# Output parts taken out of the matmul chain, and the third tile in pairs of block pairs

## The chip, the cores and the metric

The kernel runs on one core of a Trainium2 chip. The metric is the device time of one execution in microseconds (us), the median of several runs. TensorE is called PE here, VectorE DVE, ScalarE ACT, GpSimd POOL, and SyncE, which issues the transfers, SP.

## The reference

Attention inside chunks of 64 positions gives x, and x goes through a layer of two weight matrices with h*cos(h) between them, everything in f32:

```python
scores = scale * np.matmul(q_c, k_c.transpose(0, 1, 2, 4, 3))   # 8 x 8 heads, 9 chunks of 64, head size 64
scores = scores - np.max(scores, axis=-1, keepdims=True)
attn = np.exp(scores)
attn = attn / (np.sum(attn, axis=-1, keepdims=True) + 1e-09)
out = np.matmul(attn, v_c)
...
h = x @ w_in                       # x: 4608 x 512, w_in: 512 x 2048
g = h * np.cos(h)
return (g @ w_out).astype(np.float32)   # w_out: 2048 x 512
```

## The kernel before

The 4608 tokens are nine tiles of 512. Every f32 operand of the large products is split into a high and a low part, and a product is made of three matmuls: high by high, high by low, low by high. The products h = x w_in are made chunk by chunk (16 chunks `fc` of 128 hidden units), g = h cos(h) is made on ACT and DVE, split into g_hi (ACT, a cast) and g_lo (DVE or POOL, a subtraction), and multiplied by w_out into four accumulators `acc0` to `acc3`, one for each 128 tokens of the tile. One such step for one chunk and one accumulator is an output part (`out_part`, L1183): three matmuls of 128x512.

The first two tiles are made chunk by chunk. From the third tile on (`FAST = 2`) h of a block of 2x2 is made by seven products instead of eight, in Strassen's manner (A11, S3, S2, A12, A22, S1, S4), with sums and differences of x and of w_in; h is then put together with copies between banks (ACT) and additions (DVE). The third tile does this on its own two halves of 256 tokens: `single_pair` (L1630, called eight times) makes two chunks, with products of 256 columns in the halves of two PSUM banks. The later tiles are taken two at a time, with products of 512 columns: `wide_pair` (L1695) makes two chunks of both tiles; the g of the second tile of the two goes to DRAM (`gathered`) and comes back in `second_tile` (L1772).

The combinations of w_in are in DRAM (`combo`) and are streamed through seven rooms in SBUF, `w_in5` to `w_in11`, with two combinations to a room. `load_two` (L1060) fills a room with one transfer of 512 KB; in the third tile only rooms 5 to 8 are filled again (`KEPT_ROOMS`), and `product` (L1129) asks for the next filling behind the second product on a room. SP issues all transfers in one order.

What runs when: all work is written down as pieces (engine, length, what it waits for), and a list planner (`placed`, L322, called by `in_order`, L415) sorts the pieces of all engines once, by a due time for each piece from a table of numbers (`DUE_SECOND` for the stretch with the third tile and the two after it, `DUE_NEXT` for the next tiles, `DUE_LAST` for the last two). The instructions are then written in that order, and each engine keeps to it. The pieces of PE with 128-row operands are a chain: `pe` (L1555) makes each wait for the one before it, so that their order is the order in which the code makes them, and only the scores and weighted sums of the attention (matmuls of 64x64, in groups) are free to move among them. Output parts are links of this chain: `outs(n)` (L1582) puts the next n of the waiting output parts in at places that the code names, by the tuples of `PLAN` (L48) and by the arguments `after` of `single_pair` and `wide_pair`. An output part waits for g_lo of its chunk and, where it begins an accumulator, for the copy that empties that accumulator.

g_hi and g_lo have three rooms in turn (`parts_of_g`, L1592): the split of a chunk waits until the output parts on the chunk three before it are done. `chain` (L1610) makes g: a rounding on ACT, a turn on DVE, the sine on ACT, a product on DVE. `weighted_now` (L1887) puts the weighted sums of a later tile into the list.

## Time and profile before

| what | us |
|---|---|
| median of three runs | 792.22 |
| these runs | 791.0, 792.22, 794.23 |
| the profiled execution's own time | 789.22 |
| its span, first to last instruction | 787.5 |
| PE busy | 771.1 (98%) |
| DVE busy | 574.0 (73%) |
| ACT busy | 474.6 (60%) |
| POOL busy | 307.7 (39%) |

The profile is of one execution, on the only core. A time at the start of a row of the timeline counts from the span's start; what stands in brackets behind a row is how long the engine had been idle ahead of it, and which instruction ended the wait. Matmuls are pipelined: a row of a single matmul shows its whole passage, and the next one begins before that has ended. The third tile and the attention of the tiles after it lie at about 200 to 290 us, the later tiles from there to the end; the order of the instructions on PE is the same in both kernels up to about 200 us.

### The profile page before, as it was taken

The numbers are of one execution on the slowest core, as the hardware profiler recorded it, in microseconds if no ns is written. First come the engines' busy times: TensorE is split into PE (matmuls) and PEld (weight loads), VectorE is DVE, ScalarE is ACT, GpSimd is POOL, SyncE is SP. The second block draws the span as 40 slices with busy tenths as digits, with TensorE's granted clock in tenths as the row PEclk, the third lists the DMA queues.
The fourth block names the chain that finished last, engine by engine and source line by source line (L and its number), as shares of the span: only waits on it lengthen the run. The fifth ranks groups of instructions, "written<-read, shape, count | busy, mean of one in ns | idle before, by whom it ended". The sixth has DMA issues, their size and how long they took to land.

```text
span 787.5 us, 15182 instructions
## 1 busy us (share of the span) xinstructions
PE 771.1 (98%) x5818; PEld 672.4 (85%) x5818; DVE 574.0 (73%) x908; ACT 474.6 (60%) x874; POOL 307.7 (39%) x243
## 2 busy tenths in 40 slices
PE   7999999999999999999999999999999999999998
PEld 6788887888889988888888888888888888888887
DVE  6988888998898787884887868876888564463521
ACT  6999975555877666655654456544754465554422
POOL 3555537866734382211235731121245512131200
PEclk9999999999999999999999999999999999999999
DMA  9993706386886657646656349547463265553431
GB/s 343 411 416 114 242 1 235 132 318 220 310 271 198 218 188 243 239 134 217 213 150 211 117 168 322 184 150 253 145 203 108 61 222 171 190 165 128 157 98 67
DMA packets 71896, 156.18 MB, mean 198 GB/s; under 512 B 7184, under 2 KB 21776, under 8 KB 71824
## 3 DMA queue, kind: packets, MB, share of 16 engines
q1 hardware_dynamic: 71824, 155.22, 57.6%
q8 instruction: 46, 0.75, 0.4%
q14 instruction: 26, 0.21, 0.1%
HBM read 117.44 MB, written 37.75 MB: 197 GB/s over the span
## 4 chain that ended last, share of the span: by engine, by line
PE 82%; ACT 5%; DMA 5%; DVE 5%; issue 2%; POOL 0%; SPq 0%; ACTq 0%; DVEq 0%; POOLq 0%
PE acc L495 42%; PE h L495 31%; PE a L495 9%; DMA w_out<-in_w_out_dram 3%; DVE w L571 1%; ACT w L576 1%; DMA w_in<-in_w_in_dram 1%; ACT half L578 1%; DMA gathered<-w_in 1%; DMA kt<-in_kT_dram 1%; DVE m L716 0%; ACT g L895 0%; ACT g L893 0%; ACT w_out L512 0%; ACT e L728 0%
## 5 line engine op out<-in xcount | busy, mean ns | idle before, releaser
L495 PE MATMUL acc<-w_out,g_hi 128*128 128x512 f32 x1124 | 335.0, 380 | 0.0
L495 PEld LDWEIGHTS acc<-w_out,g_hi 128*128 128x128 f32 x1124 | 209.4, 189 | 29.0
L495 PE MATMUL acc<-w_out,g_lo 128*128 128x512 f32 x562 | 212.8, 379 | 0.9 <-POOL g_lo L516 0.9
L516 POOL TENSOR_TENSOR g_lo<-g,g_hi 128x512 fp32r<-128x512 f32 x75 | 108.1, 1443 | 266.0 <-ACT g_hi L512 123.2
L495 PE MATMUL h<-x,w_in 128*128 128x512 f32 (+1 forms) x864 | 199.8, 358 | 2.9 <-DVE g L1158 1.8
L495 PEld LDWEIGHTS h<-x,w_in 128*128 128x128 f32 x864 | 149.6, 190 | 24.3 <-DVE g L1158 3.0
L495 PE MATMUL h<-w_in,w_in 128*128 128x512 f32 (+1 forms) x576 | 135.9, 354 | 0.8 <-ACT h L1142 0.6
L495 PEld LDWEIGHTS acc<-w_out,g_lo 128*128 128x128 f32 x562 | 106.2, 189 | 16.4 <-POOL g_lo L516 1.3
L495 PEld LDWEIGHTS h<-w_in,w_in 128*128 128x128 f32 x576 | 99.5, 190 | 13.4 <-ACT h L1142 0.8
L512 ACT CAST g_hi<-g 128x512 fp32r<-128x512 f32 x99 | 61.2, 620 | 51.3 <-PE acc L495 32.1
L1151 DVE SCALAR_TENSOR_TENSOR g<-g,h 128x512 f32<-128x512 int32 (+1 forms) x40 | 23.1, 577 | 68.5 <-ACT g L1148 68.0
L495 PE MATMUL a<-x,w_in 128*128 128x512 f32 x288 | 70.3, 380 | 0.5 <-DVE w_in L720 0.3
L495 PEld LDWEIGHTS a<-x,w_in 128*128 128x128 f32 x288 | 54.1, 189 | 9.2 <-PE h L495 1.3
L516 DVE TENSOR_TENSOR g_lo<-g,g_hi 128x512 fp32r<-128x512 f32 x41 | 35.8, 874 | 26.0 <-ACT g_hi L512 25.4
L1155 ACT ACTIVATE g<-g 128x512 f32<-128x512 f32 (+1 forms) x72 | 41.5, 581 | 16.9 <-DVE g L1151 16.7
L1142 ACT COPY h<-h 128x512 f32<-128x512 f32 (+1 forms) x40 | 19.4, 486 | 51.7 <-PE h L495 41.3
L516 POOL TENSOR_TENSOR e<-e,z 128x512 f32<-128x512 f32 x13 | 16.9, 1308 | 44.0 <-DVE z L770 33.9
L1145 DVE TENSOR_TENSOR w_in<-h,w_in 128x512 f32<-128x512 f32 (+1 forms) x40 | 22.6, 582 | 15.4 <-PE h L495 10.6
L1155 ACT ACTIVATE w_in<-w_in 128x512 f32<-128x512 f32 x48 | 29.8, 628 | 5.4 <-DVE w_in L1151 5.3
L1158 DVE TENSOR_TENSOR g<-w_in,g 128x512 f32<-128x512 f32 x32 | 28.8, 899 | 3.5 <-ACT g L1155 2.5
L1148 ACT ACTIVATE g<-h 128x512 int32<-128x512 f32 (+1 forms) x40 | 20.5, 512 | 16.9 <-PE h L495 16.4
L571 DVE SCALAR_TENSOR_TENSOR w<-w,half 128x512 uint32<-128x512 uint32 x32 | 27.5, 862 | 3.9 <-ACT w L576 2.9
(205 smaller groups left out, 1166.6 us busy)
## 6 DMA issues: line engine op xcount, KB each, us to landing
w_in<-combo SPq DMA_DIRECT2D x112, 512.0 KB, 4.0
combo<-w_in SPq DMA_DIRECT2D x56, 256.0 KB, 3.3
gathered<-w_in SPq DMA_DIRECT2D x48, 256.0 KB, 2.5
qt<-in_qT_dram SPq DMA_DIRECT2D x36, 256.0 KB, 4.8
kt<-in_kT_dram SPq DMA_DIRECT2D x36, 256.0 KB, 5.1
w_in<-in_w_in_dram SPq DMA_DIRECT2D x16, 512.0 KB, 9.3
w_out<-in_w_out_dram SPq DMA_DIRECT2D x16, 512.0 KB, 9.6
w_in<-gathered SPq DMA_DIRECT2D x24, 256.0 KB, 2.9
```

The source lines that it names most:

```text
L495: kept(nc.tensor.matmul(*args, **kw))
L512: kept(nc.scalar.copy(out=out, in_=in_))
L516: kept(eng.tensor_tensor(out, a, b, op=op))
L571: kept(nc.vector.scalar_tensor_tensor(bits, bits, 3, low, op0=ALU.logical_shift_left, op1=ALU.bitwise_or))
L576: lambda: kept(nc.scalar.activation(w(), upper.bitcast(F32), AF.Prelu, scale=2.0 ** -(MORE // 8), alpha=-(2.0**32))),
L578: lambda: kept(nc.scalar.activation(low, lower, AF.Copy, scale=LOWEST)),
L1142: kept(nc.scalar.copy(out=out, in_=in_))
L1145: kept(nc.vector.tensor_tensor(out, a, b, op=ALU.add))
L1148: kept(nc.scalar.activation(g.bitcast(I32), h, AF.Identity, bias=0.25, scale=0.5 / math.pi))
L1151: kept(nc.vector.scalar_tensor_tensor(g, g.bitcast(I32), -2.0 * math.pi, h, op0=ALU.mult, op1=ALU.add))
L1155: kept(nc.scalar.activation(g, g, AF.Sin, bias=0.5 * math.pi))
L1158: kept(nc.vector.tensor_tensor(g, h, g, op=ALU.mult))
```

## The change

It has two parts, and new due tables for the last three stretches (1062 numbers before and 1010 now in the first of them), of which a line each:

```diff
 DUE_SECOND = (
-    -12.85, 2.21, 2.31, 3.75, 7.22, 3.78, 4.82, 4.73, 34.21, 4.92, 3.46, 22.89, 82.26, 18.21, 88.69, 755.07,
...
+    -34.98, 8.25, 2.5, -17, -0.46, -35.35, 120.61, -10.98, -53.72, 39.57, 9.53, 28.58, -9.06, 26.34, 20.94,
...
```

First, an output part is a piece of its own that waits only for its g_lo and for its accumulator. Which part is the first or the last of its accumulator is counted as the parts are made (`added`), and the copy out waits for all parts of the accumulator. `outs()` puts in all that wait; no place is named any more, in the third tile or in the wide pairs:

```diff
     def out_piece(t, fc, sub, half=None):
-        p = pe(
-            0.648 if half is None else 0.336, lambda: out_part(t, fc, sub, half), low_of.get((t, fc)),
-            acc_free.get(sub) if fc == first_fc(t) else None,
+        p = piece(
+            PE, 0.648 if half is None else 0.336, lambda: out_part(t, fc, sub, half), low_of.get(made_of(t, fc, sub)),
+            acc_free.get(sub), main=True,
         )
-        spent.setdefault((t, fc), []).append(p)
-        if fc == last_fc(t):
+        spent.setdefault(made_of(t, fc, sub), []).append(p)
+        made = asked_out.setdefault((t, sub), {None: [], 0: [], 1: []})
+        made[half].append(p)
+        to_come[t, sub, half] = to_come.get((t, sub, half), NFC if t else LAG) - 1
+        if half is not None:
+            if len(made[half]) == 2:
+                piece(ACT, 0.4, lambda: finish(t, sub, acc[sub], True, ACT, half), *made[None], *made[half])
+        elif not to_come[t, sub, half]:
...
-    def outs(n):
-        for _ in range(n):
...
+    def outs(n=None):
+        for _ in range(len(queue) if n is None else n):
             out_piece(*queue.popleft())
...
-        while any(q[:2] == back for q in queue):
-            outs(1)
```

Second, `two_pairs` (called four times) stands in for `single_pair`. It makes each of the seven products for two block pairs, in the two halves of one bank, so that the copies, additions, roundings, turns, sines and products on ACT and DVE take 512 columns at a time; the fourth bank is `a0`, the copy of d lies in `x0_3`, and two of the four g in `x0_2`:

```diff
-    def single_pair(k, after):
+    def two_pairs(q):
...
+        def prod(j, out, *deps, begin=None):
+            for i in range(2):
+                def go(i=i):
+                    if begin and not i:
+                        v[out] = begin()
+                    product(
+                        14 * q + 2 * j + i, v[out][:, i * HALF : (i + 1) * HALF], halves_x[j][:, 0], halves_x[j][:, 1],
+                        bool(begin) and not i,
+                    )
+                done[j] = product_piece(14 * q + 2 * j + i, 0.672, go, *(() if i else deps))
+            return done[j]
...
+        prod(A11, "a", *of(ha), begin=h_bank)
+        cb = piece(ACT, 0.6, copy_b, done[A11], *of(hb))
+        prod(S3, "d", *of("a1"), begin=lambda: bank("a", 1))
+        cd = piece(ACT, 0.6, copy_d, done[S3], *of("differences"))
+        prod(S2, "b", cb)
+        cc = piece(ACT, 0.6, copy_c, done[S2], *of("a0"))
+        prod(A12, "a", cb)
+        prod(A22, "c", cc)
+        prod(S1, "b", cc)
+        addc = piece(DVE, 0.69, add_c, done[A22], cd, *of("h2"))
+        addb = piece(DVE, 0.69, lambda: add(v["h3"], v["b"], v["ds"]), done[S1], cd, addc)
+        prod(S4, "b", addb)
...
+        for g, m, odd, half in (("g1", m1, 0, 0), ("g2", m2, 1, 0), ("g3", m3, 1, 1), ("g4", m4, 0, 1)):
+            low = parts_of_g(FAST, (q, odd, half), lambda g=g: v[g], m)
...
+            queue.extend((FAST, 4 * q + 2 * i + odd, 2 * half + sub) for i in range(2) for sub in range(2))
+            outs()
         return done
```

For this a room of the third tile holds the same combination of two block pairs, and `load_two` fills it with two transfers of 256 KB (56 in all) where one of 512 KB stood (28); the other 84 fillings stay as they were:

```diff
-            load(room.bitcast(F32), combos[i % len(combos)].rearrange("p n h d -> p (n h d)"))
+            if i < len(combos):
+                q, j = divmod(i, 7)
+                for n in range(2):
+                    load(room.bitcast(F32)[:, n * TOK : (n + 1) * TOK], combo(2 * q + n, j).rearrange("p h d -> p (h d)"))
+            else:
+                load(room.bitcast(F32), combos[i % len(combos)].rearrange("p n h d -> p (n h d)"))
```

The plan of the third tile, the rooms of x, and the second tile of two:

```diff
 PLAN = [
-    2, "scores", 2, "queries", (2, 0, 1, 1), (3, 0, 2, 3), (1, 0, 2, 2), "values", "scores 2", 3, (3, 0, 2, 3),
-    (3, 0, 2, 2), (1, 0, 3, 2), "weighted", 3, (1, 0, 2, 2), "weighted 2", 3, (3, 0, 2, 3),
+    "scores", "queries", "pair", "values", "scores 2", "pair", "weighted", "pair", "weighted 2", "pair",
 ]
 
-WIDE_X = ("x0_0", "x0_1", "x0_2", "x0_3", 13, 14, 15)
+WIDE_X = ("x0_0", "x0_1", 13, 14, 15, "x0_2", "x0_3")
...
-            while len(queue) > 8:
-                outs(1)
+            outs(max(0, len(queue) - 8) if t < NT - 1 else None)
+            if t < NT - 1 and fc == NFC // 2:
+                weighted_now(t + 2)
```

PE has 4668 matmuls in both kernels, with the same numbers of 256 and of 512 columns; only their banks and their order change. ACT has 37 instructions fewer and DVE 6, and SP has 28 more.

The order on PE is shown at three places. In its rows `h`, `a0` and `a1` are banks of products, `g_hi` and `g_lo` the parts of g, a number behind a name is that of the buffer, and `x3` means three alike in a row. The first place is the beginning of the third tile's products, just behind 200 us. Before, on PE, where the second two chunks begin:

```order
L495 MATMUL h_2832<-x1_1_2265,w_in5_2593 128x256 x6
L495 MATMUL h_2832<-x1_2_2266,w_in5_2593 128x256 x6
L495 MATMUL acc0_2789<-w_out0_599,g_hi_2749 128x512 x2
L495 MATMUL acc0_2789<-w_out0_599,g_lo_2750 128x512
L495 MATMUL h_2857<-x1_3_2267,w_in6_2644 128x256 x6
L495 MATMUL h_2832<-x1_0_2268,w_in6_2644 128x256 x6
L495 MATMUL h_2857<-w_in0_2269,w_in7_2667 128x256 x6
L495 MATMUL h_2857<-w_in1_2270,w_in7_2667 128x256 x6
L495 MATMUL acc1_2807<-w_out0_599,g_hi_2749 128x512 x2
L495 MATMUL acc1_2807<-w_out0_599,g_lo_2750 128x512
L495 MATMUL acc2_2817<-w_out0_599,g_hi_2749 128x512 x2
L495 MATMUL acc2_2817<-w_out0_599,g_lo_2750 128x512
```

Now, on PE, where the first four chunks begin, on the same parts of x:

```order
L491 MATMUL h_2626<-x1_1_2270,w_in5_1910 128x256 x12
L491 MATMUL acc1_2242<-w_out14_1491,g_hi_2438 128x512 x2
L491 MATMUL acc1_2242<-w_out14_1491,g_lo_2439 128x512
L491 MATMUL acc0_2238<-w_out13_1418,g_hi_2362 128x512 x2
L491 MATMUL acc0_2238<-w_out13_1418,g_lo_2363 128x512
L491 MATMUL a1_2666<-x1_2_2271,w_in6_2057 128x256 x12
L491 MATMUL h_2684<-x1_3_2272,w_in7_2060 128x256 x12
L491 MATMUL h_2626<-x1_0_2273,w_in8_2224 128x256 x12
L491 MATMUL a0_2718<-w_in0_2274,w_in9_2227 128x256 x12
L491 MATMUL h_2684<-w_in1_2275,w_in10_2389 128x256 x12
L491 MATMUL acc1_2242<-w_out15_1467,g_hi_2460 128x512 x2
L491 MATMUL acc1_2242<-w_out15_1467,g_lo_2461 128x512
```

Before, output parts stand between products that come one to four at a time, six matmuls each; now fourteen of these products (a row of x12 is two of them) come with few output parts between them, and those parts are of any accumulator and chunk that is ready.

The second place is the first group of scores behind the first of these products: `kt` and `qt` are keys and queries, and rows of one bank alternate with rows of the other. Before, on PE, the first rows of a group of 32, and its end, which is followed at once by the next 32:

```order
L495 MATMUL acc0_2789<-w_out3_859,g_hi_2850 128x512 x2
L495 MATMUL acc0_2789<-w_out3_859,g_lo_2851 128x512
L495 MATMUL h_2937<-kt_2562,qt_2561 64x64
L495 MATMUL a0_2938<-kt_2562,qt_2561 64x64
...
L495 MATMUL h_2937<-kt_2566,qt_2565 64x64
L495 MATMUL a0_2938<-kt_2566,qt_2565 64x64
L495 MATMUL h_2980<-kt_2596,qt_2595 64x64
L495 MATMUL a1_2981<-kt_2596,qt_2595 64x64
```

Now, on PE, around the border between two such groups of 32:

```order
L491 MATMUL h_2802<-kt_2573,qt_2572 64x64
L491 MATMUL a0_2803<-kt_2573,qt_2572 64x64
L491 MATMUL acc1_2850<-w_out2_771,w_in4_2800 128x512 x3
L491 MATMUL acc0_2856<-w_out2_771,w_in4_2800 128x512 x3
L491 MATMUL acc1_2850<-w_out0_599,w_in4_2800 128x512 x3
L491 MATMUL acc0_2856<-w_out0_599,w_in4_2800 128x512 x3
L491 MATMUL h_2879<-kt_2617,qt_2616 64x64
L491 MATMUL a1_2880<-kt_2617,qt_2616 64x64
```

Four output parts stand between the two groups, so that a run of 64 has become two of 32; over the whole kernel there are 34 runs of 64x64 matmuls now, and 26 before.

The third place is the end of the fifth tile, at about 450 us of the trace of before, ahead of the next two tiles' products; `w_out12` to `w_out15` are chunks of w_out, and the split of chunk 15 takes the room of that of chunk 12. Before, on PE:

```order
L495 MATMUL acc2_5186<-w_out14_1491,g_hi_5521 128x512 x2
L495 MATMUL acc2_5186<-w_out14_1491,g_lo_5522 128x512
L495 MATMUL acc3_5191<-w_out14_1491,g_hi_5521 128x512 x2
L495 MATMUL acc3_5191<-w_out14_1491,g_lo_5522 128x512
L495 MATMUL acc0_5169<-w_out15_1467,g_hi_5543 128x512 x2
L495 MATMUL acc0_5169<-w_out15_1467,g_lo_5544 128x512
L495 MATMUL acc1_5177<-w_out15_1467,g_hi_5543 128x512 x2
L495 MATMUL acc1_5177<-w_out15_1467,g_lo_5544 128x512
```

Now, on PE:

```order
L491 MATMUL acc3_5144<-w_out13_1418,g_hi_5491 128x512 x2
L491 MATMUL acc3_5144<-w_out13_1418,g_lo_5492 128x512
L491 MATMUL acc1_5170<-w_out12_1464,g_hi_5468 128x512 x2
L491 MATMUL acc1_5170<-w_out12_1464,g_lo_5469 128x512
L491 MATMUL acc1_5170<-w_out13_1418,g_hi_5491 128x512 x2
L491 MATMUL acc1_5170<-w_out13_1418,g_lo_5492 128x512
L491 MATMUL acc1_5170<-w_out15_1467,g_hi_5526 128x512 x2
L491 MATMUL acc1_5170<-w_out15_1467,g_lo_5527 128x512
L491 MATMUL acc1_5170<-w_out14_1491,g_hi_5498 128x512 x2
L491 MATMUL acc1_5170<-w_out14_1491,g_lo_5499 128x512
```

Before, the last part on chunk 12 stood 51 rows ahead of the first on chunk 15; now one part lies between the last on chunk 12 and the first on chunk 15.

At the end of the kernel the last parts were those of the second column half of `acc3` (128x256); now both halves of `acc3` come earlier, and the last part is a whole one of `acc0` (128x512, on w_out15).

## Rows read from the trace of the kernel before

**Rows 1.** From the page: the clock granted to PE in 40 slices of the span, in tenths of full speed.

```profile
PEclk9999999999999999999999999999999999999999
```

**Rows 2.** The waits of PE from 199 us to the end: the instruction that waited, the one that ended the wait, us in total, how often, the longest.

```profile
PE h L495 <- DVE g L1158: 1.8, 2, 1.1
PE acc L495 <- POOL g_lo L516: 0.9, 1, 0.9
PE h L495 <- ACT h L1142: 0.6, 1, 0.6
PE h L495 <- ACT w_in L1142: 0.3, 1, 0.3
PE a L495 <- DVE w_in L720: 0.3, 1, 0.3
PE h L495 <- DVE w_in L1158: 0.3, 1, 0.3
PE a L495 <- PE h L495: 0.2, 1, 0.2
PE h L495 <- DVE w_in L1145: 0.2, 1, 0.2
```

**Rows 3.** The timeline of PE at the beginning of the third tile: start and length in us, and in brackets the idle time ahead.

```profile
200.94 1.50 PE L495 MATMUL h<-x,w_in 128*128 128x256 f32 x12
202.27 0.60 PE L495 MATMUL acc<-w_out,g_hi 128*128 128x512 f32 x2
...
203.57 1.50 PE L495 MATMUL h<-x,w_in 128*128 128x256 f32 x12
205.68 1.60 PE L495 MATMUL h<-w_in,w_in 128*128 128x256 f32 x12 [0.61 <-ACT h L1142]
207.12 0.60 PE L495 MATMUL acc<-w_out,g_hi 128*128 128x512 f32 x2
...
209.56 1.60 PE L495 MATMUL h<-x,w_in 128*128 128x256 f32 x12
211.01 0.60 PE L495 MATMUL acc<-w_out,g_hi 128*128 128x512 f32 x2
```

**Rows 4.** The timeline of PE at the one wait for g_lo, in a stretch of output parts.

```profile
577.60 0.59 PE L495 MATMUL acc<-w_out,g_hi 128*128 128x512 f32 x2
...
578.25 0.59 PE L495 MATMUL acc<-w_out,g_hi 128*128 128x512 f32 x2
579.71 0.48 PE L495 MATMUL acc<-w_out,g_lo 128*128 128x512 f32 x1 [0.86 <-POOL g_lo L516]
```

**Rows 5.** The timeline of PE around a run of 32 scores (119.56, with two records to each 64x64 matmul) and around a run of 64 (between 197.20 and 199.54).

```profile
117.74 1.89 PE L495 MATMUL h<-x,w_in 128*128 128x512 f32 x8
119.56 1.16 PE L495 MATMUL a<-kt,qt 64*64 64x64 f32 x64
120.65 0.70 PE L495 MATMUL acc<-w_out,g_hi 128*128 128x512 f32 x2
...
197.20 0.38 PE L495 MATMUL acc<-w_out,g_lo 128*128 128x512 f32 x1
...
199.54 0.70 PE L495 MATMUL acc<-w_out,g_hi 128*128 128x512 f32 x2
```

**Rows 6.** From the page's costliest groups: the split of g, g_lo on POOL and g_hi on ACT (busy us and mean ns of one, then the idle time before).

```profile
L516 POOL TENSOR_TENSOR g_lo<-g,g_hi 128x512 fp32r<-128x512 f32 x75 | 108.1, 1443 | 266.0 <-ACT g_hi L512 123.2
...
L512 ACT CAST g_hi<-g 128x512 fp32r<-128x512 f32 x99 | 61.2, 620 | 51.3 <-PE acc L495 32.1
```

**Rows 7.** Groups of instructions of ACT from 200 to 290 us, shapes kept apart (busy us, mean ns of one): the sine at 256 and at 512 columns.

```profile
L1155 ACT ACTIVATE g<-g 128x256 f32<-128x256 f32 x16 | 6.6, 413 | 1.2 <-DVE g L1151 1.0
...
L1155 ACT ACTIVATE g<-g 128x512 f32<-128x512 f32 x7 | 4.4, 630 | 0.6 <-DVE g L1151 0.5
```

**Rows 8.** The same of DVE: the product that ends g, at 256 and at 512 columns.

```profile
L1158 DVE TENSOR_TENSOR g<-h,g 128x256 f32<-128x256 f32 x16 | 6.7, 416 | 1.3 <-ACT g L1155 1.3
...
L1158 DVE TENSOR_TENSOR g<-w_in,g 128x512 f32<-128x512 f32 x7 | 5.0, 721 | 0.3
```

**Rows 9.** DMA issues from 199 to 290 us: count, KB of each, median us from issue to landing.

```profile
w_in<-combo SPq DMA_DIRECT2D x25, 512.0 KB, 4.3
...
qt<-in_qT_dram SPq DMA_DIRECT2D x7, 256.0 KB, 4.5
```

**Rows 10.** From the page, DMA issues over the whole span: the loads of g that comes back from DRAM.

```profile
w_in<-gathered SPq DMA_DIRECT2D x24, 256.0 KB, 2.9
```

**Rows 11.** SP's queue in the third tile: start, time that the issue takes.

```profile
202.47 0.33 SPq L492 DMA_DIRECT2D w_in<-combo  x1
202.84 0.43 SPq L492 DMA_DIRECT2D qt<-in_qT_dram  x1
```

**Rows 12.** DMA issues from 779 us to the end.

```profile
out_dram<-x SPq DMA_DIRECT2D x3, 256.0 KB, 2.3
out_dram<-x SPq DMA_DIRECT2D x2, 128.0 KB, 2.1
```

**Rows 13.** The timeline of ACT from 779 to 786 us: the copies of the accumulators, a whole one at 779.94 and the last two behind 783.

```profile
779.94 0.59 ACT L512 COPY x<-acc 128x512 f32<-128x512 f32 x1 [3.48 <-PE acc L495]
...
783.20 1.04 ACT L512 COPY x<-acc 128x512 f32<-128x512 f32 x2 [0.92 <-PE acc L495]
```

**Rows 14.** The chain that ended last, from 775 us: its last piece.

```profile
783.86 0.37 ACT x L512
```

More of the change, by code (lines that the diff above doesn't have):

```diff
@@ L1175, in g_low, with made_of, columns_of @@
         two_by(by, lo, g, hi.bitcast(F32), ALU.subtract)
-    def first_fc(t):
-        return 1 if t == FAST else 0
-    def last_fc(t):
-        return NFC - 2 if t == FAST else NFC - 1
+    def made_of(t, fc, sub):
+        return (t, (fc // 4, fc % 2, sub // 2)) if t == FAST else (t, fc)
+    def columns_of(t, fc, sub):
+        a = (fc // 2 % 2) * HALF + (sub % 2) * P if t == FAST else sub * P
+        return slice(a, a + P)
+    added = {(0, sub, h): NFC - LAG for sub in range(NSUB) for h in range(2)}
     def out_part(t, fc, sub, half=None):
-        g_hi, g_lo = g_parts[t, fc]
+        g_hi, g_lo = g_parts[made_of(t, fc, sub)]
         cols = slice(None) if half is None else slice(half * DM // 2, (half + 1) * DM // 2)
         w_hi, w_lo = (crossed(w, in_halves_of_columns(t, sub), half) for w in w_parts["out", fc])
-        first, last = fc == first_fc(t), fc == last_fc(t)
+        both = [(t, sub, h) for h in range(2) if half in (None, h)]
+        first = all(not added.get(h) for h in both)
+        for h in both:
+            added[h] = added.get(h, 0) + 1
+        last = added[both[0]] == NFC
         if first:
@@ L1628, in product_piece @@
         return p
[L1630 removed]
+    def two_pairs(q):
         v = {}
[L1634 removed]
+        ha, hb = next_h(), next_h()
         halves_x = x_halves[FAST]
[L1636 to L1692 removed]
@@ new lines, in pair_of, with copy_c, add_c @@
+        def pair_of(name):
+            return x_named(name, F32)
+        def copy_b():
+            v["b"] = h_bank()
+            copy(v["b"], v["a"])
+        def copy_c():
+            v["c"] = bank("a", 0)
+            copy(v["c"], v["b"])
+        def copy_d():
+            v["ds"] = pair_of("x0_3")[:, 0]
+            copy(v["ds"], v["d"])
+        def add_c():
+            room = w_in_room(H_ROOM, F32)[:, PAD : PAD + 2 * TOK]
+            v["h2"], v["h3"] = room[:, :TOK], room[:, TOK:]
+            add(v["h2"], v["c"], v["ds"])
@@ new lines, in two_pairs, with links, begin, third @@
+        prod(S4, "b", addb)
+        def links(g, h, make, *deps):
+            def begin():
+                v[g] = make()
+                whole(v[g], v[h])
+            return chain(512, lambda: v[g], lambda: v[h], begin, *deps, port=h in ("h2", "h3"))
+        def third():
+            v["more"] = pair_of("x0_2")
+            return v["more"][:, 0]
+        w1, m1 = links("g1", "a", g_tile, done[A12], g_free.popleft())
+        w2, m2 = links("g2", "h2", g_tile, addc, w1, g_free.popleft())
@@ new lines, in two_pairs @@
+        w3, m3 = links("g3", "h3", third, addb, *of("more"))
+        w4, m4 = links("g4", "b", lambda: v["more"][:, 1], done[S4], w3)
+        readers[ha] = [m1]
+        readers[hb] = [m4]
+        readers["a0"] = [addc]
+        readers["a1"] = [cd]
+        readers["differences"] = [addb]
+        readers["h2"] = [m2, m3]
+        for g, m, odd, half in (("g1", m1, 0, 0), ("g2", m2, 1, 0), ("g3", m3, 1, 1), ("g4", m4, 0, 1)):
+            low = parts_of_g(FAST, (q, odd, half), lambda g=g: v[g], m)
+            if g in ("g1", "g2"):
+                g_free.append(low)
+            else:
+                readers.setdefault("more", []).append(low)
+            if g == "g3":
+                readers["more"] = [low]
+            queue.extend((FAST, 4 * q + 2 * i + odd, 2 * half + sub) for i in range(2) for sub in range(2))
+            outs()
@@ L1766, in wide_pair @@
         fcs = (2 * k, 2 * k + 1)
-        if k < NPAIR - 1:
-            queue.extend((t, fc, sub) for fc in fcs for sub in range(NSUB))
-        else:
-            queue.extend((t, fc, sub) for sub in range(NSUB) for fc in fcs)
+        queue.extend((t, fc, sub) for fc in fcs for sub in range(NSUB))
+        outs()
     def second_tile(u):
@@ L1990, in combined @@
             if rooms[n // 2] in KEPT_ROOMS:
-                last = (2 * len(rooms) + 1) // 7
+                last = 2 * (len(rooms) // 7) + 1
                 stored_sums[n] = k7 if last >= 7 else k6 if last >= 6 else None
@@ L2063, in attention_then_cos_ffn @@
         if not more:
[L2064 removed]
+            outs()
             close([], DUE_LAST)
```

108 lines of the change are left out of this document (23 added, 85 removed), and 286 rows, old and new, of tables (DUE_LAST, DUE_NEXT, DUE_SECOND).

## Prediction

> **What bounds the kernel now.** I read the page first: PE is busy for 98% of the span, and the granted clock is full in every slice [rows 1]. So time can be won only where PE waits, and lost only where the new order makes it wait or do more. PE's work is the same in both kernels, and the order is the same up to about 200 us; only what lies behind that counts. There the view of PE's waits gives nine, 4.6 us in all [rows 2]. That is less than they cost. In the timeline [rows 3] twelve matmuls of 256 columns take 202.27 - 200.94 = 1.33 us from their first start to the next row's. By that PE was ready at 203.57 + 1.33 = 204.90 and began at 205.68: 0.78 us, of which the view shows 0.61, because the passage of the last matmul covers the rest. And the twelve behind the wait take 207.12 - 205.68 = 1.44, 0.11 more. So a wait costs some 0.28 us beyond its row, and the nine cost 4.6 + 9 x 0.28 = 7.1 us. Twelve others take 1.45 us with no wait shown (209.56 to 211.01): such stalls are too short for the view, and I put three or four of them in the third tile, 0.4 us. **Together 7.5 us: more than that the change can't win on PE.**
>
> **The change part by part, against the profiled execution** (789.2 us, of which 787.5 are the span and 1.7 lie around it; the median of the three runs is 3.0 us above it, so the difference is carried over to 792.2).
>
> *The waits that go, -7.5.* Five of the nine are of the third tile's copies, additions and products on g, in the two halves of a bank, where one instruction lies between a product and the next one on that bank. With two block pairs in a bank there is always another half product of 0.67 us (1.33 / 2) behind which the copy runs. The other waits hang on the fixed places of output parts; a free part can fill them. I take all nine as gone and enter what is new by itself.
>
> *ACT and DVE, nothing.* 56 instructions of ACT with 256 columns, at 0.41 us like the sine, become 28 at 0.63 [rows 7]: 56 x 0.41 - 28 x 0.63 = 5.3 us less. On DVE 48 at 0.416 become 24 at 0.72 [rows 8]: 2.7 us less. PE's matmuls hide all of it, and what these engines took from PE in waits is already in the term above. Without that cover, with DVE as the bound, its 2.7 us would count in full.
>
> *Eight runs of scores cut in two, +2.8.* A run of 64 lies between 197.20 and 199.54 [rows 5]; with 0.22 us for the matmul at 197.20 (0.65 us for the three of an output part, 577.60 to 578.25 in [rows 4]) it takes 2.34 - 0.22 = 2.12. A run of 32 begins behind eight matmuls from 117.74, at 117.74 + 8 x 0.216 = 119.47, and the next row is at 120.65: 1.18. Either is followed by a pair that takes 0.70 instead of 0.59. So two runs of 32 cost 2 x (1.18 + 0.11) - (2.12 + 0.11) = 0.35 us more than one of 64. The 26 runs become 34, and nothing can hide this, since it is time on PE: 8 x 0.35 = 2.8. It is paid in the attention of all tiles behind the third.
>
> *One new wait for g_lo, +1.3.* At the end of the fifth tile the split of chunk 15 needs the room of chunk 12, and its last part is now one part ahead. The split takes 0.62 on ACT and, where the order has it, 1.44 on POOL [rows 6]: 2.06 us from the end of the part on chunk 12, which is itself 0.17 later than the next start. PE has 0.65 + 0.43 us of work before it needs g_lo. That leaves 2.06 + 0.17 - 1.08 = 1.15, and 0.1 to get going: about 1.3. The nearest row is the wait of before of the same kind, 0.86 [rows 4], or 1.1 with its 0.28. Queued behind it on PE are one more part and then the next tile's products, so it moves everything.
>
> *Other short distances, +1.3.* Going through the new order with these durations I find four places at which an instruction is ready at about the time PE needs it: g_lo of the seventh tile's last chunks (on DVE), the last S4 of a pair behind its addition, a second group of scores behind the bank h that the product on g frees, and the first products of a wide pair behind the scores. From 0 to 2.5 us together; I take 0.3 to 0.4 for each, the size of the small waits in [rows 2].
>
> *The smaller loads, +0.3.* Fourteen half products now stand nearly in a row, with four rooms filled again. A filling is asked for behind the second product on a room and is needed six half products later, 6 x 0.67 = 4.0 us, at five places; before, about eight output parts stood among seven products, so that there were 2.5 us and more to spare. A filling of 512 KB took 4.3 us in this stretch, other loads of 256 KB 4.5 [rows 9]; loads of 256 KB over the whole span took 2.9 [rows 10]. So from 0 to 5 x (4.5 + 0.7 - 4.0) = 6 us, the 0.7 for the way to SP and the other issue that stands ahead of it. The nearest row is the filling itself, 0.3 above the distance, and its first half now lands on its own: I take one wait of 0.3. SP spends two issues of 0.43 where it spent one of 0.33 [rows 11], 28 x 0.53 = 15 us more over 80 us; the stores of outputs and combinations behind it can take that.
>
> The Trainium skill speaks against this part: in "DMA: Bandwidth & Descriptors", sections "Anatomy of one DMA — SWDGE (gpsimd) path" and "Bandwidth", a transfer has a fixed cost of about 2.0 us beside its bytes, and transfers should be joined up to 1 MiB. By its fit (for POOL's queue; here SP issues) 512 KB would be an estimated 3.2 us and 256 KB 2.6, so that two one behind the other would be 5.2 us, beyond the 4.0, and this term some 5 us. The rows give 4.3 for the one and cannot say whether two overlap; it is the second rival below.
>
> *The end, +0.45.* The last piece was a half: ACT copied it in 0.37 us [rows 14] and 128 KB landed in 2.1. Now it is a whole part: 0.59 [rows 13] and 2.3 [rows 12]: 0.22 + 0.2 and little more.
>
> *What neither view shows, +0.8.* The order of before was made by the same planner and still has nine waits; the free parts depend on more instructions of other engines than a chain with fixed places. From 0 to 3 us (three waits of the size of the one for g_lo); I take one small one and a half.
>
> Sum: -7.5 + 2.8 + 1.3 + 1.3 + 0.3 + 0.45 + 0.8 = -0.5 us, so 788.7 for an execution like the profiled one and **791.7 us** for the median. A measurement of this kernel can tell about 0.5% from no change, 4.0 us: the forecast is no change.
>
> **Rivals.**
>
> *All waits vanish.* The free parts fill every hole, and only the scores and the end cost: -7.5 + 2.8 + 0.45 = -4.2, 788.0 us. For it: all that PE waits for before is shorter than two output parts. Against it: the place for g_lo, where distances leave no choice. It would be faster by just over the bound.
>
> *Fillings arrive late, slower.* In the third tile each of the five fillings with 4.0 us of distance lands 1.2 us late, the upper bound above (4.5 + 0.7 - 4.0): -0.5 - 0.3 + 6 = +5.2, 796.9 us; it decides from 4.0 us between the release of a room and the second landing. For it: the 4.5 us of 256 KB loads and a busy DMA in just this stretch. Against it: such loads come in groups there, and the filling needs its second half 0.67 us after its first.
>
> *Output parts tied to POOL.* A free part is put where the planner thinks g_lo is ready, and it counts POOL at 1.3 us where the trace has 1.44 [rows 6]. If four more parts wait as the one at 579.71, 4 x (0.86 + 0.28) = 4.6: 796.3 us. Against it: I found only two such distances in the order.
>
> That the change would not do what it says is out: the order has the free parts and the wide banks.
>
> **How the numbers follow.** The forecast has 0.66, all waits gone 0.11, late fillings 0.13, POOL 0.10. Faster than 788.2: most of the first rival and a tail of the forecast, 0.10. Slower than 796.2: the second rival, half of the third and a tail, 0.18. The rest, 0.72, is no change. Terms all at their low ends give 788.0, all at their high ends 800.7; the range 788.0 to 797.0 takes in both slower rivals and leaves out some 2 in 10.
>
> **What would show it.** In the waits of PE behind 199 us: none on ACT's copies of h and w_in in the third tile; one of about 1 us on g_lo from POOL at some 440 to 450 us; waits on `w_in` from a DMA in 200 to 290 us would be the second rival, more than two on g_lo the third. Two runs of 64x64 matmuls, 1.1 us each, where the timeline had one of 2.1. A last copy of 0.6 us and 256 KB behind it. Wrong would be: 512-wide matmuls further apart than 0.216 us without waits, or a clock below full.

## The result and the profile after

The changed kernel takes 796.93 us (median of 6 runs, 795.55 to 798.65) against 791.61 us of the kernel before (6 runs, 790.22 to 794.23): 1.0065 of its time, 95% interval 1.0043 to 1.0086. It is slower by about 5 us. The forecast was no change at 791.7 us.

The profiled execution is the slowest of its six (798.65 us, span 796.9), and the profiled one of before (789.22 us) is faster than each of the six runs that were timed, so the spans differ by 9.4 us where the medians differ by 5.3. Part of that is the clock: the mean granted clock is 0.995 in this execution and 0.996 to 0.998 in the five others, so the clock cost less in those. PE is busy for 778.3 us now, 771.1 before. Where it waits behind 199 us, in the same view as [rows 2]:

```profile
PE acc L491 <- DVE g_lo L512: 2.7, 1, 2.7
PE h L491 <- ACT h L1143: 1.9, 1, 1.9
PE acc L491 <- POOL g_lo L512: 0.6, 1, 0.6
PE h L491 <- DVE e L716: 0.6, 1, 0.6
PE acc L491 <- ACT g_hi L508: 0.3, 1, 0.3
```

Nine waits have become five (a sixth, of 0.27 us for g_hi from ACT, lies just ahead of this view, at 198.21 us). The waits on g, on w_in and on the bank `h` are gone. But two are longer than any before. The page still shows a full clock in all 40 slices, as [rows 1]; finer windows do not. Each row is a stretch of 20 us: busy us of PE, PEld, DVE, ACT, POOL with the count of instructions, then the granted clock, DMA share and GB/s:

```profile
320.00:340.00 20.00, 17.94 (x74) 14.79 (x74) 13.07 (x24) 9.18 (x16) 2.55 (x2) 0.91 0.59 194
...
620.00:640.00 20.00, 17.01 (x70) 13.95 (x69) 10.42 (x7) 6.18 (x11) 9.69 (x6) 0.91 0.09 30
640.00:660.00 20.00, 20.00 (x94) 17.51 (x94) 12.03 (x19) 12.42 (x21) 1.56 (x1) 1.00 0.68 234
```

In 320 to 340 and in 620 to 640 PE starts 74 and 70 matmuls where a full stretch of wide matmuls has 94, as the third row, and as both stretches had before. That is 20 and 24 matmuls of 0.216 us: 4.3 and 5.2 us.

To see all losses, short ones too, I took the start-to-start distance of the matmuls of 256 and 512 columns less what each takes without a stall (0.109 and 0.216 us), and the runs of 64x64 matmuls apart. Sums in us from 180 us on, for the profiled executions:

| | before | after |
|---|---|---|
| third tile, 200 to 300 us | 4.9 | 1.7 |
| 320 to 340 us | 0.0 | 4.3 |
| 440 to 480 us (end of the fifth tile) | 0.2 | 1.1 |
| 620 to 640 us | 0.0 | 5.2 |
| 180 to 200 us, and all the rest | 2.2 | 0.7 |
| runs of 64x64 with their borders | 27.3 (12 runs) | 29.6 (20 runs) |
| sum | 34.7 | 42.7 |

So the change won 3.2 of the 4.9 us in the third tile and gave back about three times that in two single places later on.

**The first place, 320 to 340 us.** PE's timeline:

```profile
327.57 0.38 PE L491 MATMUL acc<-w_out,g_lo 128*128 128x512 f32 x1
329.88 0.48 PE L491 MATMUL h<-w_in,w_in 128*128 128x512 f32 x1 [1.92 <-ACT h L1143]
...
331.48 2.77 PE L491 MATMUL h<-x,w_in 128*128 128x512 f32 x6
334.05 0.81 PE L491 MATMUL acc<-w_out,g_hi 128*128 128x512 f32 x2
334.69 0.38 PE L491 MATMUL acc<-w_out,g_lo 128*128 128x512 f32 x1
334.90 1.46 PE L491 MATMUL a<-x,w_in 128*128 128x512 f32 x6
```

Behind the wait of 1.92 us the six matmuls at 331.48 take 334.05 - 331.48 = 2.57 us instead of 6 x 0.216 = 1.30: half the clock (1.2 GHz). Full clock is back at 334.7. The copy that PE waits for, on ACT:

```profile
325.01 0.63 ACT L1149 ACTIVATE w_in<-w_in 128x512 int32<-128x512 f32 x1 [4.53 <-DMA gathered<-w_in]
...
329.25 0.57 ACT L1143 COPY h<-h 128x512 f32<-128x512 f32 x1
```

ACT stood still for 4.53 us: its rounding writes into a room whose former content, a g of the pair before, was still on its way to DRAM (`gathered`). The copy stands behind the rounding in ACT's order. And the store, on SP:

```profile
313.98 5.50 SPq L488 DMA_DIRECT2D w_in<-combo  x3
319.58 0.38 SPq L1787 DMA_DIRECT2D gathered<-w_in  x1
```

That g was complete only at 318.14: its sine had ended on ACT at 306.70, but the product that ends it stood on DVE behind instructions of the attention:

```profile
316.76 1.38 DVE L1159 TENSOR_TENSOR w_in<-w_in,w_in 128x512 f32<-128x512 f32 x1
```

Then SP was holding a filling whose room came free only at 319.13; the store behind it went out at 319.58, 1.4 us after its g was complete. It landed at 324.90, 5.3 us later, with two fillings still on their way (issued at 316.57 and 319.16, landed at 320.90 and 324.24); stores near by took 2.0 to 2.7 us. Before, the g was complete at 300.43 and the same store left at 300.46, long before anyone wanted the room:

```profile
300.46 0.33 SPq L1761 DMA_DIRECT2D gathered<-w_in  x1
```

**The second place, 620 to 640 us**, at the border between two stretches that are planned apart. PE:

```profile
627.35 0.70 PE L491 MATMUL acc<-w_out,g_hi 128*128 128x512 f32 x2 [0.34 <-ACT g_hi L508]
630.71 0.48 PE L491 MATMUL acc<-w_out,g_lo 128*128 128x512 f32 x1 [2.65 <-DVE g_lo L512]
...
631.91 1.06 PE L491 MATMUL acc<-w_out,g_hi 128*128 128x512 f32 x2
632.76 0.63 PE L491 MATMUL acc<-w_out,g_lo 128*128 128x512 f32 x1
```

and DVE, then POOL, then ACT, at that time:

```profile
625.81 1.49 DVE L512 TENSOR_TENSOR vt<-e,pts 128x512 f32<-128x512 f32 x1 [0.20 <-DVE pts L512]
627.22 3.43 DVE L512 TENSOR_TENSOR g_lo<-g,g_hi 128x512 fp32r<-128x512 f32 x2
```

```profile
626.72 1.72 POOL L512 TENSOR_TENSOR x<-pts,w_in 128x512 fp32r<-128x512 f32 x1
```

```profile
626.17 1.13 ACT L508 CAST g_hi<-g 128x512 fp32r<-128x512 f32 x2
```

The two g_lo of the seventh tile's last chunks (14 and 15) stand on DVE one behind the other and take 1.72 us each. DVE's sums for the next two tiles, ahead of them, held the first of the two by only 0.44 us (its g_hi was done at 626.78, it began at 627.22); but the first part that PE wants is on chunk 15, and its g_lo is the second: 627.22 + 3.43 = 630.65, and PE begins at 630.71. Ahead of the splits both casts stand on ACT in a row, from 626.17, where the last part on chunk 13 had given back the room that the cast of chunk 15 needs.

The eight output parts on these chunks are left over for the next stretch. There the planner knows nothing of the split any more (the pieces that made it belong to the stretch before, and `low_of` is emptied), so it takes the parts as ready, and six of the eight stand ahead of products of the next tiles that could run (e6, below, runs two of these products, twelve matmuls, there without a wait). In the chain of before, two of the eight stood behind six of these products and the other six behind the seventh:

```profile
630.81 0.59 PE L495 MATMUL acc<-w_out,g_hi 128*128 128x512 f32 x2
...
632.11 1.46 PE L495 MATMUL h<-w_in,w_in 128*128 128x512 f32 x6
```

From 631.4 to 634.8 in the changed kernel PE again runs at half the clock (0.85 us for two matmuls, 631.91 to 632.76).

Two smaller rows answer to steps of the prediction: the wait at the end of the fifth tile, and the last copy on ACT with the last transfers (issue to landing):

```profile
462.18 0.48 PE L491 MATMUL acc<-w_out,g_lo 128*128 128x512 f32 x1 [0.64 <-POOL g_lo L512]
```

```profile
792.89 0.58 ACT L508 COPY x<-acc 128x512 f32<-128x512 f32 x1 [1.36 <-PE acc L491]
```

```profile
out_dram<-x SPq DMA_DIRECT2D x3, 256.0 KB, 2.3
```

One correction to the text ahead of the prediction: scores and weighted sums are links of PE's chain too, in both kernels (they are made by `pe`). Before, everything on PE behind 200 us was one chain; now the output parts alone float.

### The profile page after: what moved, and what is told of

Read it like the earlier page. It is cut to its first block, busy times and chain, and to the rows that moved or that the text cites. A ratio compares the mean times of both kernels' runs of the same rounds, so it can differ in the third digit from the quotient of the medians.

```text
span 796.9 us, 15136 instructions
## 1 busy us (share of the span) xinstructions
PE 778.3 (98%) x5818; PEld 677.0 (85%) x5818; DVE 577.1 (72%) x902; ACT 465.6 (58%) x837; POOL 284.2 (36%) x232
## 4 chain that ended last, share of the span: by engine, by line
PE 84%; ACT 5%; DVE 4%; DMA 4%; issue 1%; SPq 1%; POOL 0%; DVEq 0%; ACTq 0%
PE acc L491 42%; PE h L491 32%; PE a L491 10%; DMA w_in<-in_w_in_dram 2%; ACT w L572 1%; ACT half L574 1%; DMA kt<-in_kT_dram 1%; SPq L488 1%; DMA gathered<-w_in 1%; DMA w_in<-combo 1%; DVE w_in L512 1%; DVE w L567 1%; ACT g L891 1%; DVE g_lo L512 0%; DVE pts L512 0%
## 5 line engine op out<-in xcount | busy, mean ns | idle before, releaser
L491 PE MATMUL h<-x,w_in 128*128 128x512 f32 (+1 forms) x960 | 228.9, 366 | 1.7 <-DVE g L892 1.1
L491 PEld LDWEIGHTS h<-x,w_in 128*128 128x128 f32 x960 | 171.3, 190 | 25.4 <-DVE g L892 2.0
L512 POOL TENSOR_TENSOR g_lo<-g,g_hi 128x512 fp32r<-128x512 f32 x60 | 84.8, 1413 | 277.0 <-ACT g_hi L508 161.8
L491 PE MATMUL h<-w_in,w_in 128*128 128x512 f32 (+1 forms) x384 | 98.4, 354 | 2.2 <-ACT h L1143 1.9
L491 PEld LDWEIGHTS h<-w_in,w_in 128*128 128x128 f32 x384 | 66.2, 190 | 11.1 <-ACT h L1143 2.3
L1156 ACT ACTIVATE g<-g 128x512 f32<-128x512 f32 x56 | 35.3, 630 | 17.7 <-DVE g L1152 17.5
L491 PE MATMUL a<-w_in,w_in 128*128 128x512 f32 (+1 forms) x192 | 41.1, 354 | 0.0
L491 PE MATMUL a<-x,w_in 128*128 128x512 f32 (+1 forms) x192 | 41.0, 353 | 0.0
L491 PEld LDWEIGHTS a<-x,w_in 128*128 128x128 f32 x192 | 33.0, 190 | 4.0
L491 PEld LDWEIGHTS a<-w_in,w_in 128*128 128x128 f32 x192 | 33.0, 190 | 3.9
```

The source lines that it names most:

```text
L491: kept(nc.tensor.matmul(*args, **kw))
L512: kept(eng.tensor_tensor(out, a, b, op=op))
L1156: kept(nc.scalar.activation(g, g, AF.Sin, bias=0.5 * math.pi))
```

## The experiments

My theory after the profile: two accidents of order, the late store and the left-over parts, cost about 4 and 5 us in the profiled execution, and without them the change would be a gain of a few us. The rivals: the cut runs of scores are what costs; or the loss is spread over the free parts, so that mending two places only moves it.

The kernels of the first six experiments take the planner's order of the changed kernel and move single pieces in it: `moves` holds (piece, place of which other piece, before or behind), and the list is then sorted again so that nothing stands ahead of what it waits for:

```diff
         ordered, carried[0] = in_order(work, *args, carried=carried[0])
-        for i, by in ordered:
-            work[i][2](*([by] if work[i][8] else []))
+        moved(ordered)
...
+    def moved(ordered):
+        place = {i: n for n, (i, _) in enumerate(ordered)}
+        for n, (i, at, add) in enumerate(moves):
+            place[i] = place[at] + add + n * 1e-5
...
```

**e1_store_first.** The one store goes ahead of the filling that held it up:

```diff
         a22 = prod(A22, "c", cc)
+        if (u, k) == (1, 1):
+            moves.append((kept_g[1], a22, -0.5))
```

> The changed kernel with one pair of transfers exchanged in SP's order: the store of g to DRAM that is ready at 318.14 us of the changed kernel's trace goes out ahead of the filling of room 7, which SP holds until 319.13. Theory (two long waits and the slower clock behind them make the loss): the store lands some 2 us earlier than 324.9, ACT's rounding follows it, and the 1.92 us that PE waited for the copy of h go down to 0.5 or less, and the 1.2 GHz stretch behind it (331 to 334 us) with them: 4.3 us by the distance of matmul starts from 320 to 340 us, so about 793 us where the changed kernel has 797. Rival (the loss is spread over the new order, and a wait removed here comes back at the next late instruction): within 1 us of 797. Second rival (the store is slow because the DMA queues are full, 5.3 us, whenever it is issued): the wait stays near 1.9 us.

Measured: 794.13 us (12 runs), 1.0042 of before, interval 1.0027 to 1.0056. That interval overlaps the one of the changed kernel, so the times alone don't tell the two apart; the trace does, and h1 against h3 below. On SP the store now stands between the fillings, and on ACT the rounding waits no longer for it, though narrowly (the store landed at 321.22, the wait ended with DVE's product at 321.30):

```profile
317.37 0.32 SPq L1812 DMA_DIRECT2D gathered<-w_in  x1
```

```profile
321.33 0.63 ACT L1150 ACTIVATE w_in<-w_in 128x512 int32<-128x512 f32 x1 [1.65 <-DVE g L1160]
```

The loss in 320 to 340 us falls from 4.3 to 0.1 us. The profile brought something I had not looked for: the wait at the second place is as long as before, yet the clock stays full behind it:

```profile
626.04 0.48 PE L492 MATMUL acc<-w_out,g_lo 128*128 128x512 f32 x1 [2.65 <-DVE g_lo L513]
626.36 0.59 PE L492 MATMUL acc<-w_out,g_hi 128*128 128x512 f32 x2
626.79 0.38 PE L492 MATMUL acc<-w_out,g_lo 128*128 128x512 f32 x1
```

Its stretch lost 3.5 us here and 5.2 in the profile of the changed kernel: the difference of 1.7 is the clock, and it doesn't fall in every execution. The profile of e1 is the fastest of its twelve runs.

**e2_parts_later.** The left-over parts behind the first two products of the next tiles:

```diff
+        if u > 1:
+            left_over[:] = range(len(work), len(work) + len(queue))
         outs()
...
+        if k == 0:
+            moves.extend((i, s3, 0.5) for i in left_over if work[i][0] == PE)
```

> The changed kernel with the eight output parts that are left over from the stretch before (chunks 14 and 15 of the fifth and the seventh tile) moved behind the first two products of the next wide pair, A11 and S3, as the old kernel had them behind products; everything else in the same order. Theory (these parts carry no wait for g_lo in the plan of the next stretch, so that the planner puts them first, and PE waits): the waits of PE for g_lo at 460 us (1.1 us lost) and at 627 to 631 us (0.34 + 2.65 us, and 2.1 us at the slower clock) go, 6.3 us together, so about 791 us. Rival (DVE and POOL are simply late with the split there, and the wait comes back on the products or behind them): 2 us or less won, 795 us or more.

Measured: 799.14 us (6 runs), 1.0093 (1.0068 to 1.0117); the wait on DVE's g_lo stayed at 2.6 us, and waits on ACT's copies rose to 4.1 in three. The edit was at fault: the range counts pieces, and the copies out of finished accumulators are among them, so that only six of the eight parts moved; of the other two, both on the late chunk 15, one stayed ahead of the products. It says nothing of the theory, except that parts moved without the copies that belong to them make waits of their own.

**e5_scores.** The eight cut runs of scores joined again, the rest as in the changed kernel:

```diff
                 1.06, go, *of(names[g][0]), *of(names[g][1]), queries_here.get((t, g))
             ))
+        moves.append((both[0], both[1], -0.5))
```

> The changed kernel with the first half of each group of scores or weighted sums moved right ahead of its second half, so that there are 26 runs of 64x64 matmuls again instead of 34. By the prediction's term (0.35 us for each run cut in two) 2.8 us less, 794 us, with the two long waits unchanged; if the first half's later readers on DVE and ACT make new waits, 796 to 799. If only the two long waits count and cut runs cost nothing: 797.

Measured: 797.77 us, 1.0092 (1.0068 to 1.0116): no difference from the changed kernel is shown, as the intervals overlap. PE's waits show why nothing was won:

```profile
PE a L492 <- DVE w_in L717: 1.2, 2, 0.7
PE a L492 <- PE h L492: 1.0, 2, 0.8
```

Between the two halves of a run there was time for the engines that empty their banks; joined, PE waits for these. In the measure of the table, the joined runs take 2.7 us less in e5's profile, and the starts lose about as much more, 2.5 us.

**e4_all.** The edits of e1, e2 and e5 together.

> The three edits together: the store ahead of the filling, the eight left-over parts behind the first two products, and the score groups whole. Theory (the three causes are separate and add): 4.3 + 6.3 + 2.8 = 13.4 us below the profiled 797, 784 to 786 us, faster than the old kernel by 0.7 to 0.9%. Rival (PE's waits only move): 790 us or more.

Measured: 801.19 us, 1.0126 (1.0101 to 1.0151). Two of its three edits had not done what they were for, so this doesn't test whether the gains add up; e7 does.

**e6_left_over.** The edit of e2 as it was meant: all eight parts and the copies out behind them, where one stretch begins behind another.

```diff
+        first = len(work)
         outs()
+        left_over[:] = range(first, len(work)) if u > 1 else ()
...
+        if k == 0:
+            moves.extend((i, s3 if work[i][0] == PE else cd, 0.5) for i in left_over)
```

> The changed kernel with all eight left-over output parts (chunks 14 and 15 of the fifth and of the seventh tile) behind the products A11 and S3 of the next wide pair, and the copies of their accumulators behind the copy of d on ACT; the kernel with that move before this one had left two parts on chunk 15 ahead of the products, and the copies out ahead of the copies that the products wait for. Theory (what cost is that these parts stand first, without distance to their g_lo): no wait for g_lo at 460 and 630 us, 1.1 + 5.2 us less than the changed kernel, about 791 us. Rival (DVE and POOL are that late with everything there, so the products or S2 wait instead): a wait of 2 us or more stays between 620 and 640 us, 795 us or more.

Measured: 793.05 us (7 runs), 1.0037 (1.0022 to 1.0052). The stretch of 620 to 640 us loses 1.05 us instead of 5.2, the clock there is full, and the first place stays (2.75 us in this execution, with a wait of 2.1 us and full clock). Behind the twelve matmuls of A11 and S3 the parts run without a wait; what is left is an addition that comes late for S4:

```profile
627.13 1.46 PE L492 MATMUL a<-w_in,w_in 128*128 128x512 f32 x6
628.43 0.59 PE L492 MATMUL acc<-w_out,g_hi 128*128 128x512 f32 x2
...
639.74 1.56 PE L492 MATMUL h<-w_in,w_in 128*128 128x512 f32 x6 [0.78 <-DVE w_in L1147]
```

The edit changes two things there: the place of the parts and their order, as the parts on chunk 14 now come first (628.43) and those on chunk 15 second (631.02). No run separates the two. And at the end of the fifth tile, whose left-over parts it moves as well, it wins nothing: the wait of 0.64 us for g_lo is gone, but S4 waits 0.78 us there too, and 440 to 480 us loses 1.75 us where the changed kernel loses 1.1.

**e7_both.** e6 and e1 together.

> The same, and the store of g ahead of the filling of room 7. Theory (the two long waits are separate, and with them gone the change gives what its waits in the third tile are worth): 797 - 6.3 - 3 (measured for the store alone) = 787.5 us, 0.3 to 0.5% under the old kernel. Rival (the order has more such places that come out when one is mended): 790 us or more.

Measured: 791.14 us (11 runs), 1.0019 (1.0004 to 1.0034). The two gains add up (1.8 and 2.2 us by the ratios of e1 and e6; 3.6 together, each with some 2 us either way), but where I expected a gain over before there is none. PE's waits behind 199 us:

```profile
PE h L492 <- DVE w_in L1147: 1.6, 2, 0.8
PE h L492 <- DVE e L717: 0.6, 1, 0.6
PE h L492 <- DVE w_in L1160: 0.6, 1, 0.6
PE acc L492 <- POOL g_lo L513: 0.3, 1, 0.3
PE h L492 <- DMA w_in<-combo: 0.2, 1, 0.2
```

In the measure of the table above it loses 5.5 us in starts (7.3 before) and spends 30.3 us in runs of 64x64 (27.3): 35.7 against 34.7. The first row is two additions that come 0.8 us late behind the moved parts. So the two places are most of the slow-down, 3.6 of 5.1 us by the ratios, and with them mended what is won in the third tile pays for most of the rest.

**h1_new_first and h2_old_first.** Do the late stretches need free parts at all? h1 has the new third tile, free parts and new table through the fifth tile, and from the sixth on the chain, the named places and the tables of before; h2 the other way round (there `fixed` holds for the third tile and for `u == 1`). The diff is that of h1.

```diff
+        if fixed[0]:
+            p = pe(length, run, low, acc_free.get(sub) if fc == 0 else None)
+        else:
+            p = piece(PE, length, run, low, acc_free.get(sub), main=True)
...
     for u in range(1, UNITS):
+        fixed[0] = u > 1
```

> The new third tile (pairs of block pairs) and the free output parts up to the fifth tile, with the new table there; from the sixth tile on the old chain, with the old tables. By the accounts of the two traces: 3.2 us of waits less in the third tile, six runs of scores cut in two, 2.1 us, and the wait for the store with its slower clock, up to 4.3 us: 1 to 3 us over the old kernel, 792 to 794 us. If the free parts of the later tiles were not to blame: 796 or more.

> The old third tile and the old chain up to the fifth tile with the old table; free output parts and the new tables from the sixth tile on. Theory (a left-over part is put first though its g_lo isn't ready): the wait at 630 us as in the changed kernel, 3 to 5 us, one at the end of the fifth tile of 1 to 6 us, since the old plan had more time for that split, two runs cut in two, 0.7, and the longer end, 0.45: 5 to 11 us over the old kernel, 796 to 802 us. Rival (only the new third tile and its transfers cost): within 2 us of the old kernel.

Measured: h1 792.15 us (10 runs), 1.0027 (1.0006 to 1.0047); h2 795.98 us (4 runs), 1.0077 (1.0055 to 1.0098). h1 has the late store and not the second place; h2 has the second place, with the same rows as the changed kernel, and the waits of before in the third tile. The wait that I expected in h2 at the end of the fifth tile, 1 to 6 us, did not come: 440 to 480 us loses 0.3 us there. In h2's profile the clock is at half from the very first matmul behind the wait, and this stretch loses 6.6 us:

```profile
629.56 0.80 PE L495 MATMUL acc<-w_out,g_lo 128*128 128x512 f32 x1 [2.65 <-DVE g_lo L516]
630.14 1.06 PE L495 MATMUL acc<-w_out,g_hi 128*128 128x512 f32 x2
631.00 0.63 PE L495 MATMUL acc<-w_out,g_lo 128*128 128x512 f32 x1
...
635.26 0.86 PE L495 MATMUL acc<-w_out,g_hi 128*128 128x512 f32 x2
```

**h3_new_then_old_store.** h1 with the store of e1.

> The new third tile and the free parts through the fifth tile, the old chain from the sixth tile on, and the store of g issued ahead of the filling of room 7. The theory: the run with the new third tile alone was at 1.0027 of the kernel before and had one wait of 1.7 us for ACT's copy at about 330 us (2.4 us with what it costs beyond its row), which stands behind this store; with the store ahead it goes, and the time is 790 us, 0.999 to 1.001 of the kernel before: no change, the waits won in the third tile being given back by seven more cuts of score runs (2.5 us). The rival, that the wait at 330 us hides another that takes its place (ACT's roundings are late for other reasons too), gives 1.002 to 1.003 as before. Faster than 0.998 would show that the clock or something else that no row shows was lost with the late store.

Measured: 788.81 us (11 runs, 788.01 to 790.96) against 790.6 us of before (15 runs): 0.9984, interval 0.9974 to 0.9995, faster than before by 1.3 us by the ratio, a little more than expected. Its interval and that of h1 lie apart, so the store is shown by the times too. It has six more runs of 64x64 than before, not seven. PE's waits behind 199 us are four, none over 0.7:

```profile
PE acc L492 <- POOL g_lo L513: 0.7, 1, 0.7
PE h L492 <- DVE e L717: 0.6, 1, 0.6
PE h L492 <- DMA w_in<-combo: 0.4, 1, 0.4
PE a L492 <- DMA w_in<-combo: 0.2, 1, 0.2
```

The sum of the table is 33.6 here (4.5 in starts, 29.0 in 18 runs), 1.1 below before.

## Why the prediction was wrong

Point by point, by its own steps, in us:

| step | predicted | measured |
|---|---|---|
| waits that go | -7.5 | -7.3 in starts and -0.7 inside runs; of the third tile's new order 1.7 come back below |
| score runs cut | +2.8 | +2.9 (29.6 - 27.3 + 0.7) |
| g_lo at the end of the fifth tile | +1.3 | +1.1 |
| g_lo of the seventh tile's last chunks, one of four short distances | +0.3 to 0.4 | +5.2 |
| the three others, and the smaller loads | +1.2 | +1.7, of which 0.4 on a load |
| the end | +0.45 | a last copy of 0.58 and 256 KB in 2.3 us, as taken |
| what neither view shows | +0.8 (0 to 3) | +4.3 for the late store, +0.7 at 198 us |

Of the 9.4 us between the spans about 0.9 is in none of these.

**The step that failed first** is the distance of the seventh tile's last g_lo. The prediction named the place and the engine and put the term at 0.3 to 0.4 us, the size of the small waits in [rows 2]; how long the way to this g_lo is, it does not work out. With one cast of 0.62 us and one split of 0.69, the time of a split on DVE where POOL was idle (638.62 us of before), from 626.17 on, g_lo would have been there at an estimated 627.48, about when PE came to it. In the trace two casts and two splits stand in a row, the splits at 1.72 us each beside POOL's sums, and it was there at 630.65. This is the same mechanism, a room given back shortly ahead of the split, that the prediction reckoned with at the end of the fifth tile, where it came out (+1.3 taken, +1.1 measured). The place cost 3.5 us at full clock (e1) and 5.2 with the fall of the clock; with the eight parts moved and put in the order of their chunks, e6, it costs 1.05 us. And the size of a wait does not bound its cost: 3 us of waiting came to 3.5, 5.2 and 6.6 us in three profiles, by the clock behind it.

**The second step** is the sentence that stores behind the fillings on SP "can take that". It looked at SP's issue time (15 us over 80) and not at what SP holds: a filling that waits for its room keeps everything behind it, and there was one store among it whose room ACT needed next, of a g that DVE had ended late. A range of 0 to 3 us for the unseen could have held only the wait, not the clock behind it. e1 and h3 show this cause.

**The rivals.** Late fillings: refuted as the cause. No row of PE's waits names a DMA in 200 to 290 us of the changed kernel. One filling was late all the same: its halves, asked for at 253.10 and 253.54, landed at 256.50 and 258.60, and the product on the second began at 258.64, so that the twelve matmuls of the two products take 1.73 us instead of 1.34:

```profile
257.68 1.90 PE L491 MATMUL h<-w_in,w_in 128*128 128x256 f32 x12
259.41 0.60 PE L491 MATMUL acc<-w_out,g_hi 128*128 128x512 f32 x2
```

That is 0.4 us at one place, as the prediction's term had it (+0.3), where the rival had 1.2 us at five. The two halves of another, asked for at 230.11 and 230.48, landed at 233.06 and 234.26, and their products began at 233.93 and 234.60: on time by 0.9 and 0.3 us. In h3 PE does wait for two fillings, 0.4 and 0.2 us: the mechanism was near, and its price small. By the fit of the Trainium skill ("DMA: Bandwidth & Descriptors", "Anatomy of one DMA — SWDGE (gpsimd) path"), which is for POOL's queue, two loads one behind the other would have taken an estimated 5.2 us. Here SP issues, and the 21 such pairs of the third tile took from 3.9 to 7.4 us (this one 234.26 - 230.11 = 4.15), on both sides of the estimate, so the trace neither bears out nor refutes that the two fixed costs add up. That the measured 796.93 us is next to this rival's 796.9 is luck, and so is that it lies just within the stated range: the rival's mechanism gave 0.4 us. Its sum also takes off the 0.5 twice; 792.2 + 5.2 is 797.4, which the range does not take in. Parts tied to POOL: refuted, one wait of 0.64 and no second one; DVE was the engine. All waits vanish: not seen, and even h3 keeps four. What the prediction named as its own refutation, "a clock below full", is what the windows show.

The changed part that pays is the third tile and the free parts behind it up to the fifth; from the sixth tile on, free parts brought nothing here, with these tables, that the chain did not have (h3 against e7: 0.9984 and 1.0019). Not shown is whether the order of the two chunks alone would have mended the second place, whether another due table would place the left-over parts better, or whether a planner that carried g_lo over the border would do so by itself.

## What to carry to other kernels

When an order of instructions is freed, look first at the borders where the planner starts anew: whatever was made ahead of the border counts as ready there, and a chain that held it back by accident is gone. For each room that is written again, follow the store that empties it back through its queue, to the instruction that this queue holds ahead of it. And don't price a wait of PE of some 2 us by its length alone: the clock behind it cost up to as much again here, and only windows finer than the page's 40 slices showed that. Nor does the view of waits show every late load.

## What the runs showed of the hardware

In some profiles the granted clock fell to half behind single waits of PE of 1.9 to 2.7 us that lay between full stretches, and was full again some us later (331.1 to 334.5 and 631.4 to 634.8 in the changed kernel, 629.0 to 635.8 in h2). Six profiles have the wait of 2.65 us at the second place. In five of them the window of 620 to 640 us shows a lower clock (0.91 in the changed kernel, e2, e4 and e5, 0.83 in h2), and in e1 it shows 1.00. Behind waits of 2.1 us (e6) and 1.7 us (h1) at the first place it stayed at 1.00. Each kernel has one profile, so how often a fall comes is not shown.

DVE and POOL slowed each other where each read two f32 tensors from SBUF: a split of 128x512 on DVE, 0.69 us where POOL was idle (638.62 us of before), took 1.72 us beside POOL's sums, and these took 1.72 us too, where POOL's own splits took from 1.27 us (620.41 of the changed kernel). The Trainium skill says in "SBUF — State Buffer", "SBUF: two separate sides", that the two share a pair of ports, which the one that starts first holds for its whole instruction. The rows agree: the two engines take turns, one pair of instructions each 1.7 us.
